# Pooled attention with a PReLU feed-forward: where the PReLU reads, who makes a copy, and how the last tile is stored

## The chip, the core and the metric

The kernel runs on one core of one Trainium2 chip. The core has a matrix engine (PE, with its weight loads PEld), a vector engine (DVE), a scalar engine (ACT), a general engine (POOL) and a queue that issues DMAs (SP). Each of them works through its own instructions in order and waits for the others by semaphores. The metric is the device time of one execution in microseconds, less being better; the time before is the median of three runs.

## The reference

Two parts are chained. First an attention over 8 batches, 8 heads, 576 positions and a head size of 64, in which keys and values are averaged over 8 neighbours, so that each query sees 72 keys. Then a feed-forward over all 4608 tokens of 512 numbers: a product with a 512 x 2048 matrix, a PReLU with one slope per hidden column, and a product with a 2048 x 512 matrix.

```python
k_p = k.reshape(B, H, Sp, pool, D).mean(axis=3)
v_p = v.reshape(B, H, Sp, pool, D).mean(axis=3)
scores = scale * np.matmul(q, k_p.transpose(0, 1, 3, 2))
attn = np.exp(scores - np.max(scores, axis=-1, keepdims=True))
attn = attn / (np.sum(attn, axis=-1, keepdims=True) + 1e-09)
x = np.matmul(attn, v_p)
...
h = x @ w_in
g = np.maximum(h, 0.0) + alpha * np.minimum(h, 0.0)
return (g @ w_out).astype(np.float32)
```

## The kernel before

The 4608 tokens are cut into 9 chunks of 512 (`CH`, `NC`), a chunk into 4 tiles of 128 tokens (`TPC`). Numbers are held as a high and a low half in 16 bits, so that each product is three matmuls: high by low, low by high, high by high.

**First feed-forward product.** For each of 16 blocks f of 128 hidden columns, `ffn1_products` (L759) runs 12 matmuls into one bank of the PSUM tile `h`; there are two such banks (`ps_h`). `ffn1_scaled` (L770) lets ACT write a scaled copy of h to an SBUF tile `t`, multiplied by `rp`, one number per hidden column. `ffn1_prelu` (L774) lets DVE take the maximum of h times `ra` and t, and write it over t; `ra` is `rp` times the slope `al`. So DVE reads the bank after ACT has. `ffn1_parts` (L779) makes the halves of g: ACT casts t to the high half (L784), POOL subtracts it from t for the low half (L787). The t tiles come from a pool of four buffers tagged "f", which the attention and the output tiles use too.

**Second feed-forward product.** `ffn2` (L817) takes a tile of 128 tokens and runs, for each f, the three matmuls of `ffn2_step` (L810) into one PSUM tile of 128 x 512 numbers. Then ACT scales it into an SBUF tile (`out_tile`, L803), and SP stores the tile's 256 KB (`store`, L808).

**The attention** of a chunk (`attention`, L304) is prepared while the chunk before it is in the feed-forward. It loads keys, queries and values, adds up neighbours (the values on POOL, L467), scales and splits, and then for each of the 4 tiles makes scores on PE, exponentials on ACT and sums on DVE; POOL multiplies by the reciprocal (L536) into `e`. The weights then go to `apad`, an SBUF tile of 128 x 2 x 8 x 128 numbers in 16 bits; two such tiles take turns. ACT casts `e` into its first 72 columns twice, once for each of the two layers l (L541). POOL puts the low halves of the weights beside them, in two pieces (L544 and L547). A transposing DMA (L552) turns `apad` into `aT`, which the mix with the values (L609) reads after all 4 tiles are there.

**The order.** Chunk 0 and the attention of chunk 1 are laid out by `_Plan`, which orders operations by hand-set ranks. For chunks 1 to 8 the loop at L911 emits the feed-forward of chunk c with the operations of the attention of chunk c + 1 in between (`_Line`), and the mix after the second output tile. The instructions of this loop are ordered at compile time by the framework's scheduler, from its own estimate of each duration (`schedule_with_timeline_sim=True`). `tc.issue_after` at L923 keeps what the line emits on an engine behind the last transpose, the last mix operations and the last output store of chunk 0 on that same engine; so on SP the loads for a chunk stand behind the transposes of the chunk before.

Of the kernel before, what the change touches and what calls it, by code (L numbers as in the profile page):

```python
# [9 lines left out]
F32 = mybir.dt.float32  # L10
I32 = mybir.dt.int32
U32 = mybir.dt.uint32
AF = mybir.ActivationFunctionType
# [7 lines left out]
SP = S // POOL  # L21
NT = B * S
DM = H * D
DFF = 2048
P = 128
CH = 512
HC = CH // 2
NC = NT // CH
NPR = H // 2
NK = DM // P  # L30
NF = DFF // P
TPC = CH // P
# [104 lines left out]
def pooled_attention_prelu_ffn(ctx: ExitStack, tc: tile.TileContext, qT, kT, vT, kN, vN, w1, w2, alpha, out):  # L137
# [5 lines left out]
    nc = tc.nc  # L143
# [9 lines left out]
    fp = ctx.enter_context(tc.tile_pool(name="fp", bufs=ROOM["f"]))  # L153
# [28 lines left out]
    al = const.tile([P, NF], F32, name="al")  # L182
# [121 lines left out]
    def attention(add, c, bs, rank, begin=False, early=False, k_pool=0, q_cuts=1, on_act=(), on_dve=(), behind=()):  # L304
# [52 lines left out]
        for j, b in enumerate(bs):  # L357
            ks, ps = kss[b], kl[b]
            if begin:
                ps = [ps]  # L360
            else:
                ps = []
                for a, z, t, ld in kl[b]:
                    if len(ps) < k_pool:
                        x = ld
                        for w, us in ((4, 1.6), (2, 1.2), (1, 0.8)):
                            def half(a=a, z=z, t=t, ks=ks, w=w):
# [4 lines left out]
                            x = add("Pool", us, half, x, rank=rank, take="f" if w == 4 and not ps else None,  # L372
                                    give=None if early or w > 1 else "big")
# [3 lines left out]
                        out=ks().rearrange("p a s -> p (a s)")[:, a:z], in_=t().rearrange("p (s w) -> p s w", w=POOL),  # L377
# [6 lines left out]
            ld, rank=rank + 0.18 * i) for i, (q, (t, ld)) in enumerate(zip(q16s[c], ql))]  # L384
# [4 lines left out]
        for i, (cols, dep) in enumerate(groups):  # L389
            r = []  # L390
            rk = rank + 2.19 * i
            x = reduce_max(add, r, lambda cols=cols: m()[:, cols], cols.stop - cols.start, *dep,
                           cap=2.0 ** 126, rank=rk)
# [8 lines left out]
            x = add("DVE", 0.2, floors, x, rank=rk)  # L402
            scs.append(add("DVE", 0.2, lambda cols=cols: recip(s()[:, cols], e()[:, cols], 13), x, rank=rk))
        if first:
            ma, ra = once(lambda: sml.tile([P, 1], F32, tag="ma", name="ma")), []
            x = add("DVE", 0.2, lambda: absmax(ma(), al), al_ld, rank=rank + RK["al"])
            x = reduce_max(add, ra, lambda: ma(), 1, x, rank=rank + RK["al"])
# [13 lines left out]
        for i, b in enumerate(bs):  # L421
            for j in range(2):
                rr, cs = slice(64 * j, 64 * j + 64), slice(SP * j, SP * j + SP)
# [8 lines left out]
                h = add("ACT", 0.53, hi, scs[0], rank=rank)  # L432
                kd.append(add("DVE", 0.6, lo, h, *kd[2 * i:], rank=rank, give="f" if j else None, two=True))
        qd = {}
        for i, (t, ld) in enumerate(ql):
            q = q16s[c][i]
            sc = lambda i=i: s()[:, 1 - i:2 - i]
            rk = rank + rks["q"] * i
            w = HC // q_cuts
            for a in range(0, HC, w):  # L440
                cs = slice(a, a + w)
# [5 lines left out]
                    out=q()[:, 1, :, cs], in0=t()[:, :, cs], scalar=sc(), in1=q()[:, 0, :, cs],  # L447
# [51 lines left out]
        for i in range(TPC):  # L499
            rk = rank + rks["sm"] + rks["sms"] * i  # L500
            ps = once(lambda: ps_s.tile([P, 2, CH], F32, tag="s", name="s"))
            mx = once(lambda: sml.tile([P, 2, 4], F32, tag="mx", name="mx", bufs=4))
            sm = once(lambda: sml.tile([P, 2, 4], F32, tag="sm", name="sm", bufs=4))
            ex = once(lambda: wp.tile([P, 2, 4, SP], F32, tag="e", name="e"))
            sv = lambda ps=ps: ps()[:, :, :4 * SP].rearrange("p b (h s) -> p b h s", s=SP)
            ap = apads[i % 2]
            x = add("PE", 0.8, lambda i=i, ps=ps: scores(c, i, ps()), *kd, qd[i], rank=rk, take="S")

            def top(i=i, mx=mx, sv=sv):
                descale(c, i)  # L510
                nc.vector.tensor_reduce(out=mx(), in_=sv(), axis=AX.X, op=ALU.max)
            x = add("DVE", 0.8, top, x, rank=rk)
            nb = once(lambda: sml.tile([P, 2, 4], F32, tag="nb", name="nb", bufs=4))
            if i in on_act:
                x = add("DVE", 0.2, lambda i=i, nb=nb, mx=mx: nc.vector.tensor_scalar(
                    out=nb(), in0=mx(), scalar1=descale(c, i), scalar2=-1.0, op0=ALU.mult, op1=ALU.mult), x, rank=rk)

                for q in range(4):
                    def exps(i=i, ex=ex, nb=nb, sm=sm, sv=sv, b=q // 2, q=q % 2):
                        for h in (2 * q, 2 * q + 1):  # L520
                            nc.scalar.activation(ex()[:, b, h], sv()[:, b, h], AF.Exp, scale=descale(c, i),
                                                 bias=nb()[:, b, h:h + 1], accum_out=sm()[:, b, h:h + 1])
                    x = add("ACT", 0.8, exps, x, rank=rk, take=None if q else "e", give="S" if q == 3 else None)
            else:
                x = add("DVE", 0.73, lambda ex=ex, mx=mx, sv=sv: nc.vector.tensor_tensor(
                    out=ex(), in0=sv(), in1=mx().broadcast_to([P, 2, 4, SP]), op=ALU.subtract),
                    x, rank=rk, take="e", give="S")
                x = add("ACT", 0.78, lambda i=i, ex=ex: nc.scalar.activation(ex(), ex(), AF.Exp, scale=descale(c, i)),
                        x, rank=rk)
                x = add("DVE", 0.73, lambda sm=sm, ex=ex: nc.vector.tensor_reduce(  # L530
                    out=sm(), in_=ex(), axis=AX.X, op=ALU.add), x, rank=rk)
            x = add("DVE", 0.2, lambda sm=sm: nc.vector.tensor_scalar(
                out=sm(), in0=sm(), scalar1=1e-9, scalar2=2.0 ** -13, op0=ALU.add, op1=ALU.mult), x, rank=rk)
            x = add("DVE", 0.25, lambda sm=sm: nc.vector.reciprocal(out=sm(), in_=sm()), x, rank=rk)  # L534
            eng, us = (nc.vector, 0.75) if i in on_dve else (nc.gpsimd, 1.25)
            x = add("DVE" if i in on_dve else "Pool", us, lambda ex=ex, sm=sm, eng=eng: eng.tensor_tensor(  # L536
                out=ex(), in0=ex(), in1=sm().broadcast_to([P, 2, 4, SP]), op=ALU.mult), x, rank=rk, two=True)
            ev_ = lambda ex=ex: ex().rearrange("p b h s -> p (b h) s")
            y = []
            for l in range(2):  # L540
                x = add("ACT", 0.67, lambda l=l, ap=ap, ev_=ev_: nc.scalar.copy(out=ap[:, l, :, :SP], in_=ev_()),  # L541
                        x, *td[i - 2:i - 1], rank=rk)
                y.append(x)
            x = add("Pool", 1.2, lambda ap=ap, ev_=ev_: nc.gpsimd.tensor_tensor(  # L544
                out=ap[:, 0, :, SP:], in0=ev_()[:, :, :LO0], in1=ap[:, 0, :, :LO0], op=ALU.subtract),
                y[0], rank=rk)
            z = add("Pool", 0.5, lambda ap=ap, ev_=ev_: nc.gpsimd.tensor_tensor(  # L547
                out=ap[:, 1, :, SP:2 * SP - LO0], in0=ev_()[:, :, LO0:], in1=ap[:, 0, :, LO0:SP], op=ALU.subtract),
                *y, rank=rk, give="e")

            def transpose(i=i, ap=ap):
                last["t"] = nc.sync.dma_start_transpose(  # L552
                    out=aT()[:, :, i * P:(i + 1) * P], in_=ap.rearrange("p l h s -> p (l h s)"))
            td.append(add("SP", 2.2, transpose, x, z, *y, rank=rk + RK["td"], take=None if i else "aT"))
# [202 lines left out]
    gs, hps, hs = {}, {}, {}  # L757
# [14 lines left out]
        nc.scalar.activation(t, hps[c, f], AF.Copy, scale=rp[:, f:f + 1])  # L772

    def ffn1_prelu(c, f):  # L774
        t = hs[c, f]
        nc.vector.scalar_tensor_tensor(out=t, in0=hps.pop((c, f)), scalar=ra[:, f:f + 1], in1=t,  # L776
                                       op0=ALU.mult, op1=ALU.max)

    def ffn1_parts(c, f, l):  # L779
# [11 lines left out]
    def out_scale(c, i):  # L791
        pr = _parts(c, i)
        key = pr[0][2] if len(pr) == 1 else (c, i)
        if key not in oss:
            t = sml.tile([P, 1], F32, tag="os", name="os", bufs=4)
            for a, z, b in pr:
                nc.vector.tensor_tensor(out=t[a:z], in0=wsc[a:z], in1=ev[b][a:z], op=ALU.mult)
            oss[key] = t
        return oss[key]

    def out_tile(c, i, ps):
        o = fp.tile([P, DM], F32, tag="f", name="o")
        nc.scalar.activation(o, ps, AF.Copy, scale=out_scale(c, i))  # L803
        return o

    def store(c, i, o):
        t0 = c * CH + i * P
        return nc.sync.dma_start(out=out[t0:t0 + P, :], in_=o)  # L808

    def ffn2_step(c, i, f, ps):  # L810
        ts_ = slice(i * P, i * P + P)
        g, w = gs[c][f], w16[2][f]
        nc.tensor.matmul(ps, g[:, 1, ts_], w[:, 0], start=(f == 0), stop=False)  # L813
        nc.tensor.matmul(ps, g[:, 0, ts_], w[:, 1], start=False, stop=False)  # L814
        nc.tensor.matmul(ps, g[:, 0, ts_], w[:, 0], start=False, stop=(f == NF - 1))  # L815

    def ffn2(c, i):  # L817
        ps = ps_o.tile([P, DM], F32, tag="o", name="o")
        for f in range(NF):
            ffn2_step(c, i, f, ps)  # L820
        store(c, i, out_tile(c, i, ps))


    GROUPS = ((0, 2), (2, 6), (6, 10), (10, NF))
# [70 lines left out]
    class _Line:  # L895
# [5 lines left out]
        def add(self, engine, us, emit, *after, **kw):  # L901
            self.ops.append(emit)
# [59 lines left out]
```

## Time and profile before

| what | us |
|---|---|
| median of 3 runs | 902.24 |
| the runs | 907.07, 900.93, 902.24 |
| the profiled execution | 903.4 |
| its span, first to last instruction | 901.7 |
| chunk 0 with loading and preparing of weights | about the first 161 |

The mean granted clock of PE was 0.985 of full speed. A page of the profile gives busy times and groups of instructions of one execution; the trace behind it can be asked for a stretch of time, for the waits of an engine, for one source line or for the instructions in order. A row of a timeline is start, duration, engine, line, operation, tiles written and read, shape and count; in brackets stands how long the engine was idle before it and what ended that. "q" behind an engine's name is its queue: the work of issuing, not of computing. Busy shares are means over stages with different limits; what counts for an edit is which wait ends last at the place that it touches.

### The profile page before, as it was taken

The numbers are of one execution on the slowest core, as the hardware profiler recorded it, in microseconds if no ns is written. First come the engines' busy times: TensorE is split into PE (matmuls) and PEld (weight loads), VectorE is DVE, ScalarE is ACT, GpSimd is POOL, SyncE is SP. The second block draws the span as 40 slices with busy tenths as digits, with TensorE's granted clock in tenths as the row PEclk, the third lists the DMA queues.
The fourth block names the chain that finished last, engine by engine and source line by source line (L and its number), as shares of the span: only waits on it lengthen the run. The fifth ranks groups of instructions, "written<-read, shape, count | busy, mean of one in ns | idle before, by whom it ended". The sixth has DMA issues, their size and how long they took to land.

```text
span 901.7 us, 11443 instructions
## 1 busy us (share of the span) xinstructions
PE 846.9 (94%) x4404; PEld 405.8 (45%) x4404; DVE 407.2 (45%) x657; ACT 430.6 (48%) x727; POOL 347.8 (39%) x375
## 2 busy tenths in 40 slices
PE   5779899989898989999989999999989999999998
PEld 4444354444344444454435444544444444444443
DVE  4889895484128520762077116621572145111110
ACT  5899984555324631563246234632464346313330
POOL 1357364376214730564055504640455027302320
PEclk9889999999999999999999999999999999999999
DMA  9686033606210360045012601260115004000000
GB/s 331 218 264 257 25 86 65 198 4 156 87 51 4 71 172 24 27 74 172 24 27 51 172 36 39 48 175 36 39 27 117 36 13 77 18 35 12 1 23 25
DMA packets 93638, 74.73 MB, mean 83 GB/s; under 512 B 77040, under 2 KB 77616, under 8 KB 93584
## 3 DMA queue, kind: packets, MB, share of 16 engines
q1 hardware_dynamic: 93584, 74.01, 29.2%
q8 instruction: 34, 0.56, 0.3%
q14 instruction: 20, 0.16, 0.1%
HBM read 45.10 MB, written 9.44 MB: 60 GB/s over the span
## 4 chain that ended last, share of the span: by engine, by line
PE 65%; DVE 11%; issue 7%; ACT 6%; DMA 6%; POOL 4%; SPq 1%; POOLq 0%; DVEq 0%; ACTq 0%
PE o L813 10%; PE o L814 10%; PE o L815 10%; PE h L766 9%; PE h L767 9%; PE h L768 9%; DMA vraw<-vT_dram 3%; POOL g L787 3%; DVE t L776 2%; DVE e L233 2%; DVE q L446 1%; PE x L609 1%; DMA nat<-kN_dram 1%; SPq L254 1%; ACT q L442 1%
## 5 line engine op out<-in xcount | busy, mean ns | idle before, releaser
L787 POOL TENSOR_TENSOR g<-t,g 128x512 f16<-128x512 f32 x144 | 166.9, 1160 | 397.7 <-ACT g L784 393.4
L776 DVE SCALAR_TENSOR_TENSOR t<-h,m,t 128x512 f32<-128x512 f32 x144 | 107.0, 744 | 308.4 <-ACT t L772 303.7
L766 PE MATMUL h<-x,w 128*128 128x512 f16 x576 | 220.0, 384 | 17.2 <-DVE t L776 13.9
L767 PE MATMUL h<-x,w 128*128 128x512 f16 x576 | 221.2, 384 | 0.0
L768 PE MATMUL h<-x,w 128*128 128x512 f16 x576 | 221.1, 384 | 0.0
L813 PE MATMUL o<-w,g 128*128 128x512 f16 x544 | 206.1, 380 | 10.7 <-POOL g L787 10.5
L814 PE MATMUL o<-w,g 128*128 128x512 f16 x544 | 206.4, 379 | 0.0
L815 PE MATMUL o<-w,g 128*128 128x512 f16 x544 | 204.4, 380 | 0.0
L772 ACT ACTIVATE t<-h,rp 128x512 f32<-128x512 f32 x144 | 97.5, 682 | 117.4 <-PE h L768 96.2
L784 ACT CAST g<-t 128x512 f16<-128x512 f32 x144 | 88.6, 615 | 99.0 <-DVE t L776 98.3
L803 ACT ACTIVATE o<-o,os 128x512 f32<-128x512 f32 x34 | 23.1, 687 | 156.3 <-PE o L815 156.3
L767 PEld LDWEIGHTS <-w 128*128 128x128 f16 x576 | 56.9, 99 | 83.4 <-issue 23.9
L813 PEld LDWEIGHTS <-g 128*128 128x128 f16 x576 | 56.3, 98 | 79.7 <-POOL g L787 13.1
L768 PEld LDWEIGHTS <-w 128*128 128x128 f16 x576 | 57.0, 99 | 69.7 <-issue 3.5
L815 PEld LDWEIGHTS <-g 128*128 128x128 f16 x576 | 56.4, 98 | 67.8 <-issue 0.3
L766 PEld LDWEIGHTS <-w 128*128 128x128 f16 x576 | 56.5, 99 | 65.9 <-issue 4.0
L814 PEld LDWEIGHTS <-g 128*128 128x128 f16 x576 | 56.4, 98 | 65.0 <-issue 0.6
L467 POOL TENSOR_TENSOR vraw<-vraw 72x512 f32<-72x512 f32 (+1 forms) x56 | 53.7, 972 | 43.0 <-DMA vraw<-vT_dram 39.2
L570 DVE SCALAR_TENSOR_TENSOR x<-x,xsc,x 128x512 f16<-128x512 f32 x36 | 26.1, 748 | 65.5 <-ACT x L566 65.5
L536 POOL TENSOR_TENSOR e<-e,sm 128x576 f32<-128x576 f32 x35 | 40.5, 1158 | 34.6 <-DVE sm L534 33.6
L541 ACT CAST apad<-e 128x576 f16<-128x576 f32 x72 | 44.9, 669 | 14.6 <-POOL e L536 12.4
L544 POOL TENSOR_TENSOR apad<-e,apad 128x448 f16<-128x448 f32 x36 | 37.3, 1035 | 17.7 <-ACT apad L541 17.6
(135 smaller groups left out, 840.6 us busy)
## 6 DMA issues: line engine op xcount, KB each, us to landing
w<-w_dram SPq DMA_DIRECT2D x16, 1024.0 KB
out_dram<-o SPq DMA_DIRECT2D x36, 256.0 KB
qraw<-qT_dram SPq DMA_DIRECT2D x17, 512.0 KB
vraw<-vT_dram SPq DMA_DIRECT2D x28, 288.0 KB
kraw<-kT_dram SPq DMA_DIRECT2D x12, 576.0 KB
kq<-kT_dram SPq DMA_DIRECT2D x2, 576.0 KB
nat<-kN_dram SPq DMA_DIRECT2D x2, 512.0 KB
nat<-vN_dram SPq DMA_DIRECT2D x2, 512.0 KB
```

What stands on the lines that cost most here:

```text
L467: nc.gpsimd.tensor_tensor(out=o, in0=y, in1=z, op=ALU.add)
L541: x = add("ACT", 0.67, lambda l=l, ap=ap, ev_=ev_: nc.scalar.copy(out=ap[:, l, :, :SP], in_=ev_()), x, *td[i - 2:i - 1], rank=rk)
L766: nc.tensor.matmul(ps, w[:, 1, ks_], x[:, 0], start=(n == 0), stop=False)
L767: nc.tensor.matmul(ps, w[:, 0, ks_], x[:, 1], start=False, stop=False)
L768: nc.tensor.matmul(ps, w[:, 0, ks_], x[:, 0], start=False, stop=(n == NK - 1))
L772: nc.scalar.activation(t, hps[c, f], AF.Copy, scale=rp[:, f:f + 1])
L776: nc.vector.scalar_tensor_tensor(out=t, in0=hps.pop((c, f)), scalar=ra[:, f:f + 1], in1=t, op0=ALU.mult, op1=ALU.max)
L784: nc.scalar.copy(out=g[:, 0], in_=t)
L787: nc.gpsimd.tensor_tensor(out=g[:, 1], in0=t, in1=g[:, 0], op=ALU.subtract)
L813: nc.tensor.matmul(ps, g[:, 1, ts_], w[:, 0], start=(f == 0), stop=False)
L814: nc.tensor.matmul(ps, g[:, 0, ts_], w[:, 1], start=False, stop=False)
L815: nc.tensor.matmul(ps, g[:, 0, ts_], w[:, 0], start=False, stop=(f == NF - 1))
```

## The change

Three edits.

- `ffn1_prelu`: in chunk 0 as before. In chunks 1 to 8 DVE takes the maximum of t times `al` and t, both in SBUF; h is not read by DVE any more. The value is the same, since t is h times `rp` and `ra` is `rp` times `al`.
- `attention`: from chunk 2 on (7 chunks, 28 tiles), the second copy of the weights into `apad` is no ACT cast of `e`, but a DMA on SP that copies the first layer's 72 columns of each head to the second layer: 128 partitions x 8 heads x 72 numbers in 16 bits, or pieces of 144 bytes, 147 KB in all.
- `ffn2`: the last output tile of the last chunk is made in two halves of 256 columns. All f for the first half, its scaling on ACT and its store; then the same for the second half. Both halves use the one PSUM tile.

```diff
@@ attention
             for l in range(2):
+                if l and c > 1:
+                    y.append(add("SP", 0.5, lambda ap=ap: nc.sync.dma_start(out=ap[:, 1, :, :SP], in_=ap[:, 0, :, :SP]),
+                                 x, rank=rk))
+                    continue
                 x = add("ACT", 0.67, lambda l=l, ap=ap, ev_=ev_: nc.scalar.copy(out=ap[:, l, :, :SP], in_=ev_()),
                         x, *td[i - 2:i - 1], rank=rk)
                 y.append(x)
@@ ffn1_prelu
-        t = hs[c, f]
-        nc.vector.scalar_tensor_tensor(out=t, in0=hps.pop((c, f)), scalar=ra[:, f:f + 1], in1=t,
+        t, h = hs[c, f], hps.pop((c, f))
+        nc.vector.scalar_tensor_tensor(out=t, in0=t if c else h, scalar=(al if c else ra)[:, f:f + 1], in1=t,
                                        op0=ALU.mult, op1=ALU.max)
@@ ffn2_step
-    def ffn2_step(c, i, f, ps):
-        ts_ = slice(i * P, i * P + P)
+    def ffn2_step(c, i, f, ps, cs=slice(0, DM)):
+        ts_, ps = slice(i * P, i * P + P), ps[:, cs]
...
+        nc.tensor.matmul(ps, g[:, 1, ts_], w[:, 0, cs], start=(f == 0), stop=False)
+        nc.tensor.matmul(ps, g[:, 0, ts_], w[:, 1, cs], start=False, stop=False)
+        nc.tensor.matmul(ps, g[:, 0, ts_], w[:, 0, cs], start=False, stop=(f == NF - 1))
@@ ffn2
+        if c < NC - 1 or i < TPC - 1:
+            for f in range(NF):
+                ffn2_step(c, i, f, ps)
+            store(c, i, out_tile(c, i, ps))
+            return
+        for a in range(0, DM, DM // 2):
+            cs = slice(a, a + DM // 2)
+            for f in range(NF):
+                ffn2_step(c, i, f, ps, cs)
+            o = fp.tile([P, DM // 2], F32, tag="f", name="o")
+            nc.scalar.activation(o, ps[:, cs], AF.Copy, scale=out_scale(c, i))
+            nc.sync.dma_start(out=out[c * CH + i * P:c * CH + i * P + P, cs], in_=o)
```

More of the change, by code (lines that the diff above doesn't have):

```diff
@@ L808, in store @@
         return nc.sync.dma_start(out=out[t0:t0 + P, :], in_=o)
-    def ffn2_step(c, i, f, ps):
-        ts_ = slice(i * P, i * P + P)
+    def ffn2_step(c, i, f, ps, cs=slice(0, DM)):
+        ts_, ps = slice(i * P, i * P + P), ps[:, cs]
         g, w = gs[c][f], w16[2][f]
-        nc.tensor.matmul(ps, g[:, 1, ts_], w[:, 0], start=(f == 0), stop=False)
-        nc.tensor.matmul(ps, g[:, 0, ts_], w[:, 1], start=False, stop=False)
-        nc.tensor.matmul(ps, g[:, 0, ts_], w[:, 0], start=False, stop=(f == NF - 1))
+        nc.tensor.matmul(ps, g[:, 1, ts_], w[:, 0, cs], start=(f == 0), stop=False)
+        nc.tensor.matmul(ps, g[:, 0, ts_], w[:, 1, cs], start=False, stop=False)
+        nc.tensor.matmul(ps, g[:, 0, ts_], w[:, 0, cs], start=False, stop=(f == NF - 1))
     def ffn2(c, i):
         ps = ps_o.tile([P, DM], F32, tag="o", name="o")
-        for f in range(NF):
-            ffn2_step(c, i, f, ps)
-        store(c, i, out_tile(c, i, ps))
+        if c < NC - 1 or i < TPC - 1:
[10 more added lines that the diff above has]
+            nc.sync.dma_start(out=out[c * CH + i * P:c * CH + i * P + P, cs], in_=o)
     GROUPS = ((0, 2), (2, 6), (6, 10), (10, NF))
```

## The prediction

> **What bounds the kernel now.** I first read the page's busy shares, then the busy time by stretch, then the waits of PE, and last the timelines of two places where PE stands still. Lines of the first two views:
>
> ```profile
> PE 846.9 (94%) x4404; PEld 405.8 (45%) x4404; DVE 407.2 (45%) x657; ACT 430.6 (48%) x727; POOL 347.8 (39%) x375
> ...
> 165.00:820.00 655.00, 632.52 (x3311) 298.46 (x3310) 267.80 (x424) 281.20 (x453) 254.46 (x272) 0.99 0.26 68
> ```
>
> The second line covers chunks 1 to 7: 655.00 us, of which PE is busy for 632.52; the later columns are PEld, DVE, ACT, POOL, then granted clock (0.99), DMA share and GB/s. PE is the bound, and no other engine is half used. So an edit can save at most what PE stands still, some 22 us in these chunks, and it saves that only where it ends one of these waits. PE's waits from 165 us on, then the first kind chunk by chunk (six stretches from 165 to 725 us), then the second kind in the first stretch (165 to 260) and in the last (820 to 902):
>
> ```profile
> PE h L766 <- DVE t L776: 12.9, 7, 2.6
> PE o L813 <- POOL g L787: 10.5, 6, 3.4
> ...
> PE h L766 <- DVE t L776: 1.6, 1, 1.6
> PE h L766 <- DVE t L776: 2.7, 2, 2.3
> PE h L766 <- DVE t L776: 1.8, 1, 1.8
> PE h L766 <- DVE t L776: 2.6, 1, 2.6
> PE h L766 <- DVE t L776: 1.8, 1, 1.8
> PE h L766 <- DVE t L776: 2.3, 1, 2.3
> ...
> PE o L813 <- POOL g L787: 4.6, 2, 3.4
> PE o L813 <- POOL g L787: 0.9, 1, 0.9
> ```
>
> (Total, times, longest.) Once a chunk, PE waits for a bank of h that the PReLU (L776) still reads; and it waits for the low half of g (L787) where the first FFN hands over to the second. The first kind in chunk 3, DVE, then ACT, then PE, then POOL:
>
> ```profile
> 368.65 0.74 DVE L776 SCALAR_TENSOR_TENSOR t<-h,m,t 128x512 f32<-128x512 f32 x1
> 369.31 2.79 DVE L233 TENSOR_SCALAR e<-pr 128x3 int32<-128x3 int32 x1
> 374.81 2.48 DVE L446 SCALAR_TENSOR_TENSOR q<-qraw,s,q 128x1024 f16<-128x1024 f32 x2 [0.37 <-ACT q L442]
> 377.21 0.74 DVE L776 SCALAR_TENSOR_TENSOR t<-h,m,t 128x512 f32<-128x512 f32 x1
> ...
> 372.51 1.09 ACT L426 ACTIVATE kbd<-ks,s 64x288 f16<-64x288 f32 x2 [2.47 <-DVE s L238]
> 373.63 2.19 ACT L442 ACTIVATE q<-qraw,s 128x1024 f16<-128x1024 f32 x2
> 375.72 1.24 ACT L772 ACTIVATE t<-h,rp 128x512 f32<-128x512 f32 x2
> ...
> 378.01 0.38 PE L766 MATMUL h<-x,w 128*128 128x512 f16 x1 [1.85 <-DVE t L776]
> ...
> 367.44 1.84 POOL L467 TENSOR_TENSOR vraw<-vraw 72x512 f32<-72x512 f32 x2
> 369.24 1.15 POOL L787 TENSOR_TENSOR g<-t,g 128x512 f16<-128x512 f32 x1
> ```
>
> ACT reads the bank from 375.72 (two L772 in 1.24 us, the first done near 376.4). The PReLU starts at 377.21, behind the long L446 on DVE, ends at 377.95, and PE goes on at 378.01. So the bank is held 1.57 us after ACT is done with it.
>
> **The change part by part. A, the PReLU from t.** In chunks 1 to 8 L776 takes t, in SBUF, instead of h, in PSUM; instructions stay 128 in number. The bank is then free when L772 ends. With all else in place each wait shrinks by at most 1.57: 1.57 of the 1.6; 1.57 and the small 0.4 of the 2.7; 1.57 each of 1.8, 2.6, 1.8 and 2.3. Sum: 1.57 x 6 + 0.4 = 9.8 us. The ends are 0, if the time comes back as another wait, and 12.9, all of it. I take 9.8, because the hold was read at a typical place. What is late next is the second L772, near 377.0, whose bank PE needs one f step later, so it is covered.
>
> Against it stands the price of the PReLU with two operands in SBUF. The lines of DVE's kinds, minimum/median/maximum in ns:
>
> ```profile
> L776 DVE SCALAR_TENSOR_TENSOR t<-h,m,t x144: 692/750/779, 67.6 to 872.7; 128x512 f32<-128x512 f32 x144
> L691 DVE SCALAR_TENSOR_TENSOR w<-v,s,w x16: 700/746/1757, 105.1 to 147.1; 128x512 f16<-128x512 f32 x16
> L233 DVE TENSOR_SCALAR e<-pr x10: 153/1662/2795, 17.2 to 731.8; 128x3 int32<-128x3 int32 x7, 128x2 int32<-128x2 int32 x2, 128x1 int32<-128x1 int32 x1
> ```
>
> L691 is the same operation with both inputs in SBUF: median 746 against 750, so the work itself costs nothing more. But L691 and L233, both SBUF alone, have maxima 1.0 us over the median and 2.6 over the minimum, while the 144 PReLUs from PSUM never pass 779. The long L233 above lies on a stretch in which POOL runs without a pause. I conclude that such operations wait for POOL, and that the PReLU will start to. At 368.65 it would wait behind the POOL operations shown. I cost that at nothing there: the L233 behind it waits for the same POOL work anyway, and the next L787 needs this PReLU's result, so POOL must pause and let DVE in. Elsewhere the PReLU's followers (L784, L787) have slack until the hand-over. If that cover is gone, it costs what the slower rival says.
>
> [...]
>
> **B, the second copy by DMA.** For chunks 2 to 8, prepared during chunks 1 to 7, 28 of 72 ACT copies L541 go, and SP gets 28 copies ahead of the transposes, which then wait for the landing. SP issues in order and behind the last transpose stand the next chunk's loads, vraw last. ACT, SP, then POOL, then PE in chunk 3:
>
> ```profile
> 404.87 1.25 ACT L541 CAST apad<-e 128x576 f16<-128x576 f32 x2 [0.20 <-POOL e L536]
> ...
> 407.06 1.80 SPq L552 DMA_TRANSPOSE aT<-apad  x1
> 408.96 1.57 SPq L254 DMA_DIRECT2D kraw<-kT_dram  x2
> 411.80 0.35 SPq L254 DMA_DIRECT2D vraw<-vT_dram  x1
> ...
> 406.61 0.43 POOL L547 TENSOR_TENSOR apad<-e,apad 128x128 f16<-128x128 f32 x1
> 419.52 3.06 POOL L467 TENSOR_TENSOR vraw<-vraw 72x512 f32<-72x512 f32 x3 [3.70 <-DMA vraw<-vT_dram]
> 422.55 1.15 POOL L787 TENSOR_TENSOR g<-t,g 128x512 f16<-128x512 f32 x1
> ...
> 423.75 0.39 PE L813 MATMUL o<-w,g 128*128 128x512 f16 x1 [1.15 <-POOL g L787]
> ...
> 198.09 1.75 DMA v<-v
> 210.49 4.48 DMA aT<-apad
> ```
>
> Here PE waits at the hand-over because the last g of the chunk (422.55) stands on POOL behind three vraw additions, which waited for vraw. ACT saves some 0.6 us a tile (half of the 1.25), which lies beside PE and ends none of the waits above: worth nothing by itself. The copy's landing is not in the trace. Its nearest rows are the small SBUF copy v<-v (1.75 us) and the transpose (4.48 us); it has many short pieces, so I put it between them, at 2.6. The first L541 ends near 405.5, so apad is whole at about 408.1 instead of 407.04, when L547 ends: 1.1 us later (0.2 and 3.0 at the ends). Transpose, loads and vraw move by as much; the mix, which the code puts inside the second FFN, leaves room for it; the vraw additions don't.
>
> What that does at the hand-over hangs on POOL's order, which is fixed at compile time from the scheduler's own estimate of when vraw is there. With the order kept, five chunks (1 to 5) pay 1.1 each: +5.5. But a vraw that the scheduler too holds for later gets fewer additions ahead of the last g, and each takes about 1.0 (3.06 / 3), which gives the 1.1 back. If it is held for later than all three, the wait is gone: of the 10.5 us, less 0.9 in the last chunk and 1.2 of the 4.6 in chunk 1 (4.6 less its longest, 3.4), that is 8.4. So B lies between -8.4 and +15 (3.0 x 5). I take 0, as the shift and the dropped addition are of one size.
>
> **C, the last tile in halves.** 48 matmuls of 512 columns become 96 of 256: the same streaming. The end, as it is now, then ACT's row for 128 columns and PE's restart after an earlier output:
>
> ```profile
> 897.54 0.38 PE L815 MATMUL o<-w,g 128*128 128x512 f16 x1
> 898.02 0.69 ACT L803 ACTIVATE o<-o,os 128x512 f32<-128x512 f32 x1 [9.67 <-PE o L815]
> 898.73 0.33 SPq L808 DMA_DIRECT2D out_dram<-o  x1
> ...
> L206 ACT ACTIVATE pd<-ident,m x42: 384/394/417, 12.2 to 710.3; 128x128 bf16<-128x128 bf16 x42
> ...
> 877.04 0.38 PE L813 MATMUL o<-w,g 128*128 128x512 f16 x1 [0.19 <-ACT o L803]
> ```
>
> A half on ACT takes 0.49 (a third of the way from 0.394 at 128 columns to 0.69 at 512), 0.2 less at the end. From the store's issue to the end of the span (901.7) are 2.97 us; beyond the issue's 0.33 and the 1.75 of a small copy some 0.9 are moving, and half of that is 0.4. Gain 0.6. Against it: both halves lie in one PSUM tile, and 877.04 shows a matmul held until ACT has read what it overwrites. If the second half waits for ACT's read of the first, PE loses 0.26 (897.54 to 898.02 less one matmul's 0.22) + 0.49 + 0.06 (as from 377.95 to 378.01) = 0.8. Net +0.2; the ends are -0.6 and +0.8, and I take the wait.
>
> [...]
>
> **Sum.** The profiled run took 903.4 us (span 901.7 and 1.7 around it), 1.2 over the median of 902.24. 903.4 - 9.8 + 0 + 0.2 = 893.8, which against the median is 892.6.
>
> **The rivals.** *The hand-over clears too:* POOL's order puts the last g ahead of vraw: 892.6 - 8.4 = 884.2. For it: the copy's landing lies in the schedule as well as on the chip. Against it: three additions' worth is more than the 1.1 that I find. *The gain is given back at the hand-over:* order kept, +5.5, so 898.1, and with the landing at its upper end 892.6 + 15 = 907.6; or A ends no wait because the same chain holds PE elsewhere: 902.4. For it: four of the seven chunks already wait there for vraw. *Slower, the PReLU waits for POOL:* each PReLU among the attention's POOL work delays DVE in series with the last transpose; passed on in five chunks it outweighs A and reaches +1% (911.3) from 3.7 us a chunk. Two waits a chunk as long as L233's (2.6 each) give 892.6 + 5 x 5.2 = 918.6. For it: L233's median of 1662. Against: POOL is busy 254 of 655 us, and a PReLU that waits also thins POOL's work, as the next L787 needs its result.
>
> **How the numbers follow.** Chances: forecast 0.38, hand-over clears 0.22, given back 0.25, slower 0.15. A measurement of this kernel tells about 1% from no change, 9 us. The forecast lies just beyond that bound (893.2); I give it 0.24 faster and 0.14 the same. Faster 0.24 + 0.22 = 0.46; same 0.14 + 0.25 = 0.39; slower 0.15. The range reaches from the cleared hand-over to the upper end of the given-back case, 883 to 907; it leaves out the slower rival and little else.
>
> **What would show it.** A is right if PE's wait at L766 names ACT t L772 or falls from 12.9 to about 3 us; the port's part if L776's maximum goes far over 779 ns. B shows in the time between the last apad of a chunk and vraw's landing, and in PE's wait at L813 (10.5 now): near 10 for the forecast, 2 if it clears, 16 and more if it is given back. C shows as a gap of 0.8 us on PE before the second half. The prediction is wrong if DVE's and POOL's order changes so that attention itself ends later.

## The result and the profile after

The changed kernel took 872.38 us, median of 4 runs (872.12 to 874.49); the kernel before, beside it on the same chip, 902.62 (900.93 to 907.07). The ratio is 0.966, 95% interval 0.963 to 0.970: 30 us less. Forecast were 892.6 and a range of 883 to 907: the direction was right, the size a third of what came, and the time lies below the range. The profiled execution took 872.6 us, its span 870.4; PE's mean granted clock was 0.994, before 0.985.

First the page's busy row of the changed kernel, then its busy time from 165 us to 790 us, which is nearly the stretch that was shown of the kernel before; columns as there.

```profile
PE 836.8 (96%) x4452; PEld 409.4 (47%) x4452; DVE 426.2 (49%) x657; ACT 413.7 (48%) x700; POOL 371.1 (43%) x375
```

```profile
165.00:790.00 625.00, 623.12 (x3310) 297.18 (x3309) 286.39 (x424) 264.22 (x425) 278.12 (x272) 1.00 0.31 78
```

PE does nearly as many matmuls in these 625.00 us (3310) as in the 655.00 before (3311), and stands still for 1.9 us of them where it was 22.5. Over the whole execution its idle time fell from 54.8 us (901.7 - 846.9) to 33.6 (870.4 - 836.8), that is by 21.2, and its busy time by 10.1, although the matmuls are the same work. So two things went: waits, and matmuls that took longer than they need. The waits first: PE's own from 165 us on, in total, times and longest.

```profile
PE o L817 <- POOL g L791: 1.7, 2, 1.4
PE o L817 <- ACT o L833: 0.6, 1, 0.6
PE h L770 <- ACT t L776: 0.2, 1, 0.2
PE o L817 <- ACT o L807: 0.2, 1, 0.2
```

(After the change L766 is L770, L772 is L776, the PReLU L776 is L780, the low half of g L787 is L791, and L813 is L817.) The waits for a bank of h that took 12.9 us are one of 0.2, and it names ACT. Those at the hand-over to the second product fell from 10.5 to 1.7. The forecast let the first kind shrink to about 3 us and left the second as it was. The chain of waits says the same by engine, first before, then after:

```profile
PE 65%; DVE 11%; issue 7%; ACT 6%; DMA 6%; POOL 4%; SPq 1%; POOLq 0%; DVEq 0%; ACTq 0%
```

```profile
PE 85%; DVE 6%; ACT 4%; DMA 3%; issue 1%; SPq 1%; ACTq 0%; DVEq 0%
```

DVE and POOL, which made up 15% of the chain, have 6%.

The matmuls that took longer: the kernel before, busy time by short stretches around two of its waits. The last columns are granted clock, DMA share and GB/s.

```profile
227.00:231.00 4.00, 4.00 (x43) 2.11 (x42) 0.84 (x2) 1.30 (x2) 0.24 (x1) 1.00 0.67 186
231.00:235.00 4.00, 0.57 (x5) 0.08 (x3) 2.06 (x3) 1.26 (x2) 4.00 (x5) 1.00 0.00 0
235.00:239.00 4.00, 4.00 (x11) 1.51 (x12) 0.42 (x1) 2.41 (x4) 0.51 (x1) 0.57 0.23 83
239.00:243.00 4.00, 4.00 (x20) 1.81 (x19) 0.33 (x1) 2.31 (x6) 0.00 (x0) 1.00 0.14 52
...
471.00:475.00 4.00, 4.00 (x16) 1.66 (x15) 0.66 (x2) 1.05 (x3) 2.31 (x2) 0.57 0.02 4
```

PE waits from 231 to 235 us for the low half of g, and in the four microseconds after that its granted clock is 0.57: 11 matmuls where the next four hold 20. The same follows waits of 2.5 us (ended at 282.23) and 2.7 us (ended at 470.38), both for a bank of h. Each time some 3.4 us ran at half rate, which costs 1.7; three times, 5.1 us. None of this is there after the change: its clock is 1.00 over the whole stretch above. (Chunk 0 has such stretches too, with a clock of 0.95 before and 0.97 after, but chunk 1 began at 161.7 and 161.1 us, so little of that reached the end.)

How many such stretches there are differs between executions of one and the same program. `c_only` below is the kernel before up to its last tile, with the same order of operations on PE, ACT, DVE and POOL; its trace has one stretch at half rate behind 165 us in place of three. In 39 timed runs of the kernel before, beside the experiments below, the granted clock was 0.988 in the mean (0.982 to 0.992), in the four of the changed kernel 0.9925. One less the clock, times the run's time, is 10.9 and 6.5 us. So half rate makes up at most some 4.4 of the 30 us over many runs, though this pair of traces shows more.

**The place that the forecast argued from**, in chunk 3 after the change: DVE, then ACT, then PE.

```profile
351.93 2.22 DVE L780 SCALAR_TENSOR_TENSOR t<-t,al 128x512 f32<-128x512 f32 x1 [1.80 <-ACT t L776]
...
356.37 1.07 DVE L233 TENSOR_SCALAR e<-pr 128x3 int32<-128x3 int32 x1
...
355.15 0.69 ACT L776 ACTIVATE t<-h,rp 128x512 f32<-128x512 f32 x1 [0.34 <-PE h L772]
...
357.86 1.09 ACT L426 ACTIVATE kbd<-ks,s 64x288 f16<-64x288 f32 x2 [2.02 <-DVE s L238]
358.97 2.19 ACT L442 ACTIVATE q<-qraw,s 128x1024 f16<-128x1024 f32 x2
361.57 0.68 ACT L776 ACTIVATE t<-h,rp 128x512 f32<-128x512 f32 x1
...
358.56 0.38 PE L817 MATMUL o<-w,g 128*128 128x512 f16 x1
359.85 0.38 PE L770 MATMUL h<-x,w 128*128 128x512 f16 x1
```

ACT still does the attention's `kbd` and `q` between two scaled copies, from 357.86 to 361.16, so a bank waits there for ACT; PE has no wait, since steps of the second product (358.56) stand between those of the first. DVE's PReLU of 2.22 us, against 0.74 before, holds nobody on PE.

**The hand-over** of the same chunk, on POOL:

```profile
395.21 1.16 POOL L791 TENSOR_TENSOR g<-t,g 128x512 f16<-128x512 f32 x1 [1.28 <-ACT g L788]
397.64 1.16 POOL L791 TENSOR_TENSOR g<-t,g 128x512 f16<-128x512 f32 x1 [1.27 <-ACT g L788]
...
409.75 3.64 POOL L467 TENSOR_TENSOR vraw<-vraw 72x512 f32<-72x512 f32 x4 [10.95 <-DMA vraw<-vT_dram]
```

Before, the last g of this chunk stood behind three vraw additions and began when the last of them ended, at 422.55; now it ends 10.95 us before the first. From POOL's rows in both traces, the end of a chunk's last g and the start of the first vraw addition near it:

| chunk | before: last g ends, vraw begins | after: last g ends, vraw begins |
|---|---|---|
| 1 | 234.9, 230.8 | 224.0, 237.2 |
| 2 | 331.9, 328.3 | 310.9, 322.2 |
| 3 | 423.7, 419.5 | 398.8, 409.7 |
| 4 | 517.6, 513.4 | 487.7, 497.5 |
| 5 | 609.8, 605.6 | 576.0, 587.9 |

So in all five chunks the last g was behind vraw, by about 4 us, and now it is 10 to 13 us ahead. Why it comes earlier is seen in chunk 5. Its first product ran from 540.9 to 602.0, 61.1 us, and now from 517.7 to 571.8, 54.1. The scheduler lets steps of the second product of the chunk before (three matmuls each, 0.65 us) run between those of the first. Between the first and the last matmul of the first product stand, for chunks 1 to 8 and counted in the executed order, without the 32 steps of two output tiles that PE does behind the first block in some chunks (some of the expectations below count these too):

| kernel | steps of the second product inside the first |
|---|---|
| before | 25, 22, 22, 20, 22, 21, 24, 26 |
| after | 15, 15, 15, 15, 15, 14, 16, 22 |

A bank that comes free late is bridged with more such steps. That is no lost work, but it draws out the first product: in chunk 5, 7 steps more (4.5 us) and PE's pause of 2.0 for the bank there, from matmul to matmul (1.8 in the list of waits), make up 6.5 of the 7.0 us. And 7 us later the last g meets vraw on POOL.

### The profile page after: what moved, and what is told of

It is laid out like the page before. It is cut to its first block, busy times and chain, and to the rows that moved or that the text cites. A ratio compares the mean times of both kernels' runs of the same rounds, so it can differ in the third digit from the quotient of the medians.

```text
span 870.4 us, 11545 instructions
## 1 busy us (share of the span) xinstructions
PE 836.8 (96%) x4452; PEld 409.4 (47%) x4452; DVE 426.2 (49%) x657; ACT 413.7 (48%) x700; POOL 371.1 (43%) x375
## 4 chain that ended last, share of the span: by engine, by line
PE 85%; DVE 6%; ACT 4%; DMA 3%; issue 1%; SPq 1%; ACTq 0%; DVEq 0%
PE o L817 13%; PE o L819 13%; PE o L818 13%; PE h L770 12%; PE h L771 12%; PE h L772 12%; PE x L613 2%; DMA qraw<-qT_dram 1%; DMA nat<-kN_dram 1%; PE s L602 1%; PE s L603 1%; PE s L604 1%; DVE t L780 1%; PE h L817 1%; PE h L818 1%
## 5 line engine op out<-in xcount | busy, mean ns | idle before, releaser
L791 POOL TENSOR_TENSOR g<-t,g 128x512 f16<-128x512 f32 x144 | 171.9, 1195 | 329.0 <-ACT g L788 327.8
L780 DVE SCALAR_TENSOR_TENSOR t<-t,al 128x512 f32<-128x512 f32 x128 | 128.7, 1007 | 269.1 <-ACT t L776 259.8
L770 PE MATMUL h<-x,w 128*128 128x512 f16 x576 | 218.3, 379 | 4.7 <-DVE w2e L233 1.9
L771 PE MATMUL h<-x,w 128*128 128x512 f16 x576 | 218.3, 379 | 1.1 <-DVE x L574 1.0
L772 PE MATMUL h<-x,w 128*128 128x512 f16 x576 | 218.3, 379 | 0.0
L817 PE MATMUL o<-w,g 128*128 128x512 f16 (+1 forms) x560 | 208.1, 373 | 2.5 <-POOL g L791 1.7
L818 PE MATMUL o<-w,g 128*128 128x512 f16 (+1 forms) x560 | 208.8, 373 | 0.0
L819 PE MATMUL o<-w,g 128*128 128x512 f16 (+1 forms) x560 | 205.6, 373 | 0.0
L776 ACT ACTIVATE t<-h,rp 128x512 f32<-128x512 f32 x144 | 97.9, 681 | 59.6 <-PE h L772 58.9
L807 ACT ACTIVATE o<-o,os 128x512 f32<-128x512 f32 x33 | 22.5, 688 | 165.6 <-PE o L819 165.6
L817 PEld LDWEIGHTS <-g 128*128 128x128 f16 x592 | 57.9, 98 | 69.0 <-POOL g L791 2.7
L467 POOL TENSOR_TENSOR vraw<-vraw 72x512 f32<-72x512 f32 (+1 forms) x56 | 56.6, 1028 | 77.8 <-DMA vraw<-vT_dram 66.8
L819 PEld LDWEIGHTS <-g 128*128 128x128 f16 x592 | 57.9, 98 | 66.5
L818 PEld LDWEIGHTS <-g 128*128 128x128 f16 x592 | 57.9, 98 | 65.5 <-issue 1.3
L772 PEld LDWEIGHTS <-w 128*128 128x128 f16 x576 | 56.3, 98 | 68.7 <-issue 1.6
L770 PEld LDWEIGHTS <-w 128*128 128x128 f16 x576 | 56.3, 98 | 65.0 <-issue 0.6
L536 POOL TENSOR_TENSOR e<-e,sm 128x576 f32<-128x576 f32 x35 | 46.2, 1321 | 12.6 <-DVE sm L534 12.2
L548 POOL TENSOR_TENSOR apad<-e,apad 128x448 f16<-128x448 f32 x36 | 40.8, 1134 | 16.0 <-ACT apad L545 16.0
L545 ACT CAST apad<-e 128x576 f16<-128x576 f32 x44 | 28.9, 670 | 24.9 <-POOL e L536 13.9
## 6 DMA issues: line engine op xcount, KB each, us to landing
kraw<-kT_dram SPq DMA_DIRECT2D x12, 576.0 KB
kq<-kT_dram SPq DMA_DIRECT2D x2, 576.0 KB
```

The lines of the kernel that those rows point to most:

```text
L467: nc.gpsimd.tensor_tensor(out=o, in0=y, in1=z, op=ALU.add)
L770: nc.tensor.matmul(ps, w[:, 1, ks_], x[:, 0], start=(n == 0), stop=False)
L771: nc.tensor.matmul(ps, w[:, 0, ks_], x[:, 1], start=False, stop=False)
L772: nc.tensor.matmul(ps, w[:, 0, ks_], x[:, 0], start=False, stop=(n == NK - 1))
L780: nc.vector.scalar_tensor_tensor(out=t, in0=t if c else h, scalar=(al if c else ra)[:, f:f + 1], in1=t, op0=ALU.mult, op1=ALU.max)
L791: nc.gpsimd.tensor_tensor(out=g[:, 1], in0=t, in1=g[:, 0], op=ALU.subtract)
```

## The experiments

Ratios are to the kernel before, timed beside each of them on the same chip, with 95% intervals. A shortened diff stands with each.

### The three edits alone

The PReLU from t alone (`a_only`):

```diff
-        t = hs[c, f]
-        nc.vector.scalar_tensor_tensor(out=t, in0=hps.pop((c, f)), scalar=ra[:, f:f + 1], in1=t,
+        t, h = hs[c, f], hps.pop((c, f))
+        nc.vector.scalar_tensor_tensor(out=t, in0=t if c else h, scalar=(al if c else ra)[:, f:f + 1], in1=t,
```

> The PReLU from t alone; the weights' second copy stays on ACT and the last tile whole. Theory H (the early release of the bank of h is what pays, and it also takes the steps of the second product out of the first, so that the hand-over clears): 873 to 878 us, PE's wait for DVE at the first product near 1 us, the wait for the low half of g near 2 us. Rival V (the hand-over clears because the DMA copies move vraw in POOL's order): only the bank's waits go, 888 to 893 us, and the wait for the low half of g stays near 10 us.

Measured: 873.49 us (872.36 to 875.30), ratio 0.972 (0.968 to 0.976). PE's waits from 165 us on:

```profile
PE h L766 <- ACT t L772: 2.5, 1, 2.5
```

This edit by itself brings most of the change or all of it: 25 us by its ratio, and all but 1 by the times themselves (873.49 and 872.38). The wait at the hand-over is gone with it, though nothing of the attention's loads was touched: the last g ends 4 to 7 us ahead of vraw (in chunk 5 at 579.6, vraw at 584.0), and 15 to 17 steps, 22 in chunk 8, stand in the first product. So the hand-over hung on the bank as well.

The copy by DMA alone (`b_only`):

```diff
+                if l and c > 1:
+                    y.append(add("SP", 0.5, lambda ap=ap: nc.sync.dma_start(out=ap[:, 1, :, :SP], in_=ap[:, 0, :, :SP]),
+                                 x, rank=rk))
+                    continue
```

> The DMA copies alone. Theory H: the bank's waits stay at 11 to 14 us, the time within 1% of before, 895 to 906 us. Rival V: the wait for the low half of g falls from 10.5 to about 2 us and the time is 890 to 894 us. The order at compile time has 19 to 24 steps of the second product inside the first in chunks 1 to 7, where before it alternates between 22 and 52.

Measured: 893.02 us (888.43 to 898.19), ratio 0.993 (0.991 to 0.996). Its waits:

```profile
PE h L770 <- DVE t L780: 10.0, 7, 2.0
PE o L817 <- POOL g L791: 6.8, 4, 3.2
```

By itself the copy is a small gain. The steps inside the first product are about as many as before (24, 20, 21, 19, 21, 21, 24, 26), but vraw comes later, so that the last g is ahead of it in chunks 1, 2 and 4 and behind one addition in chunks 3 and 5. The wait at the hand-over is 3.7 us shorter. That for the bank is 2.9 shorter, but `c_only`, next, has 2.3 of this without any edit at that place. The forecast had reckoned with just this, that a later vraw drops additions ahead of the last g.

The last tile in halves alone (`c_only`):

```diff
+        for a in range(0, DM, DM // 2):
+            cs = slice(a, a + DM // 2)
+            for f in range(NF):
+                ffn2_step(c, i, f, ps, cs)
+            o = fp.tile([P, DM // 2], F32, tag="f", name="o")
```

> The last tile in halves alone. Both theories: within 1 us of before; PE pauses 0.8 us between the halves and the end after the last matmul is 0.6 us shorter.

Measured: 900.85 us (896.87 to 902.42), ratio 1.001 (0.999 to 1.003): no difference. The pause between the halves is 0.79 us, and from the last matmul's start to the end of the span pass 3.70 us in place of 4.16. Its waits:

```profile
PE h L766 <- DVE t L776: 10.6, 7, 2.1
PE o L813 <- POOL g L787: 10.5, 6, 3.4
```

Up to the last tile nothing was edited here, and the operations have the same order as before. So the difference between 12.9 and 10.6 us at the bank is that between two executions, and a difference of that size in this row between two kernels shows nothing by itself.

### The bank held again

All three edits, and after each PReLU from chunk 1 on DVE reads one column of h, into a tile that nobody uses (`hold_bank`). DVE's work on t and its inputs from SBUF stay as in the changed kernel; the bank is again held until DVE is there, at 0.15 us for each read.

```diff
+        if c:
+            nc.vector.tensor_scalar(out=y1[:, f:f + 1], in0=h[:, :1], scalar1=1.0, scalar2=None, op0=ALU.mult)
```

> All three edits, but in chunks 1 to 8 DVE reads one column of h after the PReLU, so that the bank is held as long as before. Theory H: the gain of the PReLU from t is lost, the time is that of the copies and the halves alone, 893 to 905 us, with PE's wait for DVE back at 10 us or more. Rival (reading t from SBUF is itself what pays, in DVE's work or in the order): 872 to 880 us.

Measured: 904.33 us (898.85 to 909.90), ratio 1.006 (1.003 to 1.009). Its waits:

```profile
PE h L770 <- DVE y L783: 12.5, 7, 2.3
PE o L819 <- POOL g L793: 9.9, 4, 3.9
```

The whole gain is gone, and both waits are back at the sizes that they had before (12.9 and 10.5), the second without any edit at the hand-over, though 7.7 of its 9.9 us now lie in chunks 3 and 5. The additional reads are 128 x 0.15 = 19 us of DVE, which is under half busy. From ACT's end to the end of DVE's last instruction that the bank waits for pass 1.27 us in the mean, 1.12 before. The steps inside the first product are again 23, 21, 21, 19, 21, 21, 24 and 26, and in chunks 3 and 5 the last g is again behind a vraw addition (in chunk 3 it ends at 416.3, vraw begins at 413.9). So the release of the bank, and neither where DVE takes its operand from nor the copy, is what pays.

The kernel is also 11 us slower than `b_only` (893.02), which has the same copy and releases the bank as late. The trace, of the fastest of the ten runs (898.85), shows part of that: 24 of the 128 PReLUs take over 1 us, none in `b_only`, 14 us more on DVE in all; the waits at the hand-over are 3.1 us longer, and those for the bank 2.5, which is about the difference between two executions. So where PE does wait for the bank, the time that a PReLU waits for POOL may reach PE. This was not shown: it was not measured apart from the read itself, and the granted clock differs too, 0.983 in the mean of the ten runs against 0.989, which by the estimate above (one less the clock, times the run's time) is some 5 us.

### The same order with and without the release

If the mixed-in steps bridge the hold, it must cost more where they can't be mixed in. Two kernels fix the order: the second product of a chunk is emitted behind the last matmul of its first product, in the kernel before (`order_only`), and with the PReLU from t (`a_order`).

```diff
-            nc.tensor.matmul(ps, w[:, 0, ks_], x[:, 0], start=False, stop=(n == NK - 1))
+            last["h"] = nc.tensor.matmul(ps, w[:, 0, ks_], x[:, 0], start=False, stop=(n == NK - 1))
...
-            ffn2(c, i)
+            with tc.issue_after(last["h"].ins):
+                ffn2(c, i)
```

> The kernel before, with the matmuls of the second product put behind the last matmul of the first product in each of the chunks 1 to 8 (none mixed in, where before 22 to 58 are). Theory H1 (the early release pays by itself; the order only follows): PE has nothing to do while a bank is held, so its wait for DVE grows to 20 us or more, the wait for the low half of g is near 0, and the time is 895 to 915 us. Theory H2 (the order pays, the hold as such is small): 873 to 882 us.

> The PReLU from t alone, with the second product put behind the first in the same way, so that both kernels of this pair mix nothing in. Theory H1: 872 to 880 us, 15 us or more below its pair, with PE's wait for the bank below 5 us. Theory H2: within 5 us of its pair.

Measured: `order_only` 940.21 us, ratio 1.043 (1.040 to 1.046); `a_order` 911.00, ratio 1.012 (1.009 to 1.015). The waits of the first, then of the second:

```profile
PE h L766 <- DVE t L776: 52.1, 19, 7.8
```

```profile
PE h L766 <- ACT t L772: 26.7, 9, 5.1
```

With no steps mixed in on either side, the release is worth 29.2 us (940.2 - 911.0), and the rows differ by 25.4. And where DVE holds the bank, PE waits 52 us without mixed-in steps in place of 12.9: the waits of the kernel before show only what the scheduler had not bridged. About half of the 52 stays when DVE's read is gone. That `a_order` would come to 872 to 880, with less than 5 us of waiting, was a miss: one wait of 3.7 to 5.1 us stays in each of the chunks 1 to 6, and this time ACT is the holder. ACT's rows ahead of 377.40, where PE has waited 3.75 us:

```profile
373.47 1.09 ACT L426 ACTIVATE kbd<-ks,s 64x288 f16<-64x288 f32 x2
374.59 2.19 ACT L442 ACTIVATE q<-qraw,s 128x1024 f16<-128x1024 f32 x2
376.68 1.24 ACT L772 ACTIVATE t<-h,rp 128x512 f32<-128x512 f32 x2
```

The copy of h stands behind 3.3 us of the attention's work on ACT. In the changed kernel ACT does the same (357.86 to 361.16 above), and mixed-in steps hide it. So some mixing is needed still, and it is worth some 36 us with the bank released (1.012 less 0.972, of 902).

`order_only` shows one thing more. It releases the bank as late as the kernel before, and yet it has no wait at the hand-over: the last g ends 5 to 10 us ahead of vraw in chunks 1 to 5. In chunk 5 its first product takes 54 us, as in the changed kernel, with 61 before.

### The hand-over by itself

The kernel before, with POOL's part of the attention kept behind the last g of the chunk before (`g_ahead_of_vraw`):

```diff
-            nc.gpsimd.tensor_tensor(out=g[:, 1], in0=t, in1=g[:, 0], op=ALU.subtract)
+            last["g"] = nc.gpsimd.tensor_tensor(out=g[:, 1], in0=t, in1=g[:, 0], op=ALU.subtract)
...
+        g15 = last["g"]
...
-                  tc.issue_after(last["o"].ins)):
+                  tc.issue_after(last["o"].ins), tc.issue_after(g15.ins)):
```

> The kernel before, with the additions of vraw held behind the last g of the chunk before on POOL (the attention's operations on POOL are put behind that L787). If the hand-over's waits came from vraw standing ahead of the last g, those of chunks 2, 3 and 5 (2.4, 1.2, 1.4 us) and the long one of chunk 1 (3.4) go, 8.4 us in all; the bank's waits stay at 10 to 13 us; the time is 890 to 896 us. If they came from the late end of the first product alone, the time stays within 3 us of before.

Measured: 886.01 us (885.21 to 887.65), ratio 0.984 (0.980 to 0.987). Its waits:

```profile
PE h L766 <- DVE t L776: 9.8, 7, 2.0
PE o L813 <- POOL g L787: 1.8, 2, 0.9
```

The wait for g falls from 10.5 to 1.8, so the vraw additions ahead of the last g were its cause. The steps inside the first product stay (25, 20, 22, 20, 22, 21, 24, 26), and so does most of the wait for the bank. The 15 us are more than these 8.7, and the time is lower than the 890 to 896 expected. In this trace the bank's waits are 3.1 us shorter and no stretch at half rate is left after 165 us, but `c_only` has 2.3 and two stretches less than before without an edit there. By the clock of all its runs (0.992) half rate accounts for at most 3.8 of the 15 us; the rest was not found. The hand-over alone, set right by the order on POOL, was thus worth half of what the change brought.

### Without the copy, and with two tiles at the end

`a_and_c` is the changed kernel without the copy by DMA; `two_tiles` is the changed kernel whose second half has a PSUM tile of its own; `a_c_two_tiles` is both.

```diff
         for a in range(0, DM, DM // 2):
+            if a:
+                ps = ps_o.tile([P, DM], F32, tag="o", name="o")
```

> The whole change without the DMA copies. If the copies are worth nothing once the bank is released early: within 2 us of the changed kernel's 872.4, so 871 to 875 us. If they still relieve ACT or POOL's order: 876 us or more.

> The whole change with the second half of the last tile in a PSUM tile of its own. If PE's pause of 0.8 us is the wait for ACT's read of the same tile: no pause between the halves, the span 0.8 us shorter than the changed kernel's 870.4, about 871.6 us. If the pause has another cause: unchanged.

> The PReLU from t and the last tile in halves in two PSUM tiles, without the DMA copies. If the copies are worth nothing and the two tiles save the pause: 871 to 873 us, like the changed kernel's 872.4 within the measurement's uncertainty.

| kernel | us (runs) | ratio, 95% |
|---|---|---|
| changed kernel | 872.38 (872.12 to 874.49) | 0.966 (0.963 to 0.970) |
| `a_and_c` | 872.86 (871.45 to 873.23) | 0.968 (0.966 to 0.971) |
| `two_tiles` | 873.68 (873.14 to 875.14) | 0.970 (0.967 to 0.972) |
| `a_c_two_tiles` | 872.77 (871.35 to 874.32) | 0.969 (0.964 to 0.973) |

These four can't be told apart, and no version tried beats the changed kernel. Once the bank is released, the copy by DMA is worth nothing that can be measured, although alone it was a small gain: what it shortened is gone already. The second tile removes the pause (the longest step between two matmuls of the last tile is 0.11 us in place of 0.90), and yet the 871.6 expected was not seen; in its profile `two_tiles` has a wait for ACT, in chunk 1, that the changed kernel's lacks:

```profile
PE h L770 <- ACT t L776: 2.5, 1, 2.5
PE o L817 <- POOL g L791: 0.6, 1, 0.6
```

Up to the last tile the two kernels have the same order of operations on PE, ACT, DVE and POOL, so this wait comes and goes with the execution and not with the edit. The same holds for `a_only` and `a_c_two_tiles`, which have it, and `a_and_c`, which does not. What in an execution decides it is open.

## Why the prediction was right in direction and wrong in size

**What bounds the kernel** was right: PE, with no more to be had than where it stands still. But "at most what PE stands still, some 22 us in these chunks" left out PE's time at half rate, which the row showed as a clock of 0.99: 1.7 us behind each of three waits in that execution.

**Step A failed, and in its upper end.** "The ends are 0 [...] and 12.9, all of it" took PE's listed waits at the bank for all that the hold costs, and the order of instructions on either side of it for given. Measured alone, A is worth 25 us (0.028 x 902). The mechanism named was right: `hold_bank`, which adds to the changed kernel only the read that holds the bank, takes the gain back. The term was mis-sized in three ways:

- The waits at the bank went whole, 12.7 us (12.9 - 0.2) and not 9.8: 2.9 more, which is hardly above the 2.3 between two executions. The second holder, ACT, which was called covered, keeps PE waiting for up to 5.1 us where nothing is mixed in (`a_order`); it is the mixed-in steps that cover it, and not the f step between.
- The hand-over cleared by A: 8.8 us (10.5 - 1.7). The forecast had this as a rival, at 884.2, with the copy by DMA as its cause. The copy alone gets 3.7 of the 10.5, and without it, in `a_only`, the wait is gone. `g_ahead_of_vraw` shows that POOL's order is the cause of the wait. That A turns this order because the first product ends 7 us earlier is read from the rows of POOL and PE; `order_only` agrees, where the product is as short with the bank still held. No number of mixed-in steps but zero was set by itself.
- The half rate behind the waits went with them: 5.1 us in chunks 1 to 8 of these two traces, and at most 4.4 by the clocks of all runs.

The forecast's sum for the profiled execution was 893.8; less 2.9, 8.8 and 5.1 that is 877.0, and 872.6 were measured. Of the 4.4 us left, 0.6 are chunk 1's earlier start; the rest was not followed.

**The price of two operands in SBUF** ("the port's part" in the forecast) was rightly costed at nothing for this kernel, and rightly seen on DVE. The PReLU after the change, from chunk 1 on and in chunk 0, as minimum, median and maximum in ns:

```profile
L780 DVE SCALAR_TENSOR_TENSOR t<-t,al x128: 701/788/2715, 164.7 to 839.6; 128x512 f32<-128x512 f32 x128
L780 DVE SCALAR_TENSOR_TENSOR t<-h,m,t x16: 739/744/769, 67.7 to 113.7; 128x512 f32<-128x512 f32 x16
```

With both operands in SBUF it takes up to 2715 ns; from PSUM it never passes 769. Its mean is 1007 ns against 744 before, so 128 x 0.263 = 34 us more on DVE, and PE waits for DVE in no listed row. So the mechanism of the slower rival did come, and it was not passed on: the PReLU is not what PE waits for any more, and g is ready 10 us or more before vraw. That it waits for POOL is shown by the rows of the two engines: all 50 of the 128 that take over 1 us begin while a POOL instruction runs, and the 49 beside which POOL does nothing never pass 753 ns. In 43 of the 50 the time is what that POOL instruction still had to run plus 0.55 us; the other seven waited for a vraw addition behind it as well. Why it waits there was not shown. That PE nevertheless waits 0 us for DVE from 165 us on shows that a blocked engine need not be a cost; in `hold_bank`, where PE still waits for the bank (12.5 us), it may be one.

**Step B** came to nothing, as forecast, but by another way. The landing was put too low: SP's queue in chunk 3, and SP's waits for the copies from 165 us on:

```profile
392.67 1.10 SPq L542 DMA_DIRECT2D apad<-apad  x1
396.46 1.97 SPq L556 DMA_TRANSPOSE aT<-apad  x1
398.48 1.45 SPq L254 DMA_DIRECT2D kraw<-kT_dram  x2
...
401.68 0.82 SPq L254 DMA_DIRECT2D vraw<-vT_dram  x2
```

```profile
SPq L556 <- DMA apad<-apad: 72.2, 28, 3.9
```

From the copy's issue to the transpose pass 3.8 us here (3.0, 3.9 and 3.7 for the three other tiles of the chunk, 2.9 to 5.2 for all 28), against 2.6 estimated, between 1.75 and 4.48. It didn't matter, since the last g no longer stands behind vraw. That POOL's order could turn on small shifts was seen for B ("what that does at the hand-over hangs on POOL's order") and valued from -8.4 to +15; the same doubt was not applied to A, which moves far more of the schedule.

**Step C** was right in the wait that it took; its gain at the end does not come in every trace. PE and ACT at the end of the changed kernel:

```profile
861.32 0.47 ACT L833 ACTIVATE o<-o,os 128x256 f32<-128x256 f32 x1 [4.55 <-PE o L819]
861.84 0.27 PE L817 MATMUL o<-w,g 128*128 128x256 f16 x1 [0.62 <-ACT o L833]
...
866.97 0.27 PE L819 MATMUL o<-w,g 128*128 128x256 f16 x1
867.33 0.47 ACT L833 ACTIVATE o<-o,os 128x256 f32<-128x256 f32 x1 [5.54 <-PE o L819]
```

A half takes ACT 0.47 us (0.49 forecast); the pause is 0.79 us between PE's matmuls less the time of one, 0.62 in the row (0.8 forecast); from the last matmul's start to the end of the span pass 3.43 us (870.4 - 866.97) in place of 4.16 (901.7 - 897.54), a gain of 0.7 (0.6 forecast). But the same halves take 3.70 us there in `c_only` and 4.14 in `a_and_c` and `a_c_two_tiles`, where nothing is gained. The wait that was taken is there, and it goes with the tile: in `two_tiles` PE has no wait for the scaling of the first half.

## What to carry to other kernels

Where a scheduler fills the gaps, a buffer that is held too long can cost more than the waits that are left in the profile (25 us here, with 12.9 listed): the bridging work draws out its stage (here 20 to 26 mixed-in steps, 14 to 16 after in all chunks but the last) and comes back as a wait elsewhere. When such an edit is priced, look for what the stage's end just misses (here the last g, 4 us behind vraw), and let the gain's upper end take in every wait that hangs on it, and PE's half-rate time behind them (5.1 us in this pair of traces). Two traces with the same order up to the last tile differ here by 2.3 us in a row of waits (12.9 and 10.6), so look at several before a small difference is called an effect. An engine that is blocked more may cost nothing (34 us on DVE, and no listed wait of PE for it), while a buffer that is released earlier may free a wait elsewhere (PE's for POOL, 10.5 to 1.7 us).

## What the hardware showed unexpectedly

PE's granted clock falls behind some short waits and not behind others of nearly the same length. In the trace of the kernel before, matmuls of 512 columns stand 0.427 us apart in place of 0.216 (a granted clock of 0.50) in three stretches between 165 us and PE's last matmul. They begin at 235.60, 283.38 and 471.12 us, and each lasts 3.41 us. PE's pauses of 2 us or more in the same part of that trace, read from the starts of its matmuls (from one to the next, less the 0.22 us of one):

| PE stands still until | us | half rate follows from |
|---|---|---|
| 234.99 | 3.59 | 235.60 |
| 282.23 | 2.48 | 283.38 |
| 331.97 | 2.45 | no |
| 378.01 | 2.01 | no |
| 470.38 | 2.71 | 471.12 |
| 656.13 | 2.45 | no |

So two pauses of 2.45 us cost no more than themselves, and one of 2.48 us was followed by 1.7 us of lost rate. Their lengths differ by 0.03 us; the places where they fall differ more. The stretches at half rate begin 47.79 and 187.73 us apart, which is 14.0 and 55.0 times the 3.413 us that each lasts. If that trace is cut into steps of 3.413 us from 235.60 on, in both directions, PE stood still for 2.81, 2.26 and 2.68 us in the steps just ahead of the three stretches (pauses over 0.1 us added up), and for 2.01 us or less in every other step from 165 us on. Each pause of 2.45 us lies across two steps there, with 1.65 and 1.76 us in the first. In the trace of the changed kernel the longest pause after 165 us is 1.53 us, and no half rate follows until PE's last matmul. That is what these two traces show, with three stretches in one of them; how far it holds for other executions was not shown.
